# Score matmuls of a decode attention step as four 32-column tiles of the PE array instead of zero-padded 128-column weights

## The chip, the cores and the metric

One core of one Trainium2 chip. The metric is the device time of one execution in microseconds; the kernel before takes 766.4 us (median of 3 runs, 766.21 to 766.55). PE is the matmul engine (TensorE), PEld its weight loads, DVE is VectorE, ACT ScalarE, POOL GpSimd, SP SyncE. The profile counts DMA shares over the core's 16 DMA engines.

## The reference, cut to what matters

Two tokens go through layer norm, a gated attention over the last 4096 positions of a cache of 32768, and a small MLP gate; then come all gradients. Eight key/value heads serve 32 query heads, four each.

```python
W = 4096                                        # of Sk = 32768
k = k_cache[:, :, Sk - W:, :]; v = v_cache[:, :, Sk - W:, :]
scores = einsum("bhqd,bhkd->bhqk", q, k) * Dh**-0.5
p = softmax(scores); o = einsum("bhqk,bhkd->bhqd", p, v)
out = x + (o @ wo) * silu(mlp(xn))              # and the gradients of x, k_cache, v_cache, wq, wo, w1, b1, w2, b2
```

The gradients of the two caches have the caches' full size (2 x 8 x 32768 x 128, bf16). Seven eighths of each are zeros, since only the last 4096 positions are used. These zeros have to be written: they are the bulk of the kernel's traffic.

## The kernel before

The zeros leave as large DMAs from a zeroed tile. POOL issues all regions but one on the software queue, and none of these waits for compute; the last region goes out on SP's queue, after the last result.

```python
sw_fill.append(nc.gpsimd.dma_start(out=v, in_=zs))               # L101, in zf()
...
for qi in range(ZQ - 1):                                         # 31 of 32 regions of 7.34 MB
    ...
        r = zf(*zparts[qi], r, n, rows, rep)
...
last = nc.sync.dma_start(out=out_6..., in_=dw1_st)               # the last result of the compute chain
with tc.issue_after(last.ins):
    fin = nc.sync.dma_start(out=v, in_=zs)                       # the 32nd region
tc.add_manual_dep(fin.ins, sw_fill[-2].ins.name, ...)            # and not before the last fill but one has landed
```

Attention runs in four rounds (two batches, two sets of NP = 4 key/value heads). A round loads 4 MB of V and of K, computes `dp` from V and the scores `s` from K (eight *score passes* in all, two per round), then the softmax, and overwrites the loaded tiles with the cache gradients, which are stored. A score pass takes 16 groups: eight 128x128 transposes, one evacuation (the copy from PSUM, where this kernel's matmuls write, to a ring of four buffers in SBUF, from which they read) by DVE or ACT, and four matmuls, one per head. All heads add into one 128-row accumulator: head `pr` and position group `g` own four of its rows. The weights that put them there are a 128-column window on a zero tile with the head's four query columns in it, so every head's matmul writes zeros on the rows of the other three.

```python
ZO = R - REP                                    # R = 128, REP = 4
ZW = NP * (ZO + R)
zz = const.tile([P, 2 * ZW], BF16, name="zz")   # zeros, with the query (zq) or output-gradient (zdo) columns
nc.vector.memset(zz[:], 0.0)
...
def scores(out_ps, nat, zbuf):
    n = 0
    for half in range(NH):                      # NH = 2
        for g in range(G):                      # G = 8
            tp = ps_t.tile([P, CH, P], BF16, tag="pt")        # 2 buffers in PSUM
            for j in range(CH):                 # CH = 8
                nc.tensor.transpose(tp[:, j, :], nat[:, g * CC + half * CH + j, :], pperm...)      # L384
            tF = tring[:, n % 4 * CH * R:(n % 4 + 1) * CH * R]
            tT = tF.rearrange("p (c b k) -> p c b k", c=CH, b=NP)
            evac(tF, tp..., eng=("act" if n % 4 == 3 else "dve"))
            n += 1
            for pr in range(NP):
                o = ZO - (pr * RB + REP * g)
                nc.tensor.matmul(out_ps[:, half * 256:(half + 1) * 256], lhsT=zbuf[:, pr, o:o + R],
                                 rhs=tT[:, :, pr, :], start=(g == 0 and pr == 0), stop=(g == G - 1 and pr == NP - 1))  # L391
```

## Time and profile before

| | before |
|---|---|
| time | 766.4 us |
| profiled span | 764.5 us |
| bytes moved by DMA | 326.73 MB, of them 227.55 MB on the software queue (nearly all zeros) |
| mean DMA rate | 427 GB/s |
| PE / DVE / ACT busy | 52% / 36% / 28% |
| last compute | 711 us |

First the page of the kernel before: engine totals; the DMA row, which gives the busy share of each fortieth of the span in tenths; the rate in each; and one queue with packets, MB and share of the 16 engines' time.

```profile
span 764.5 us, 9399 instructions
PE 399.7 (52%) x4118; PEld 261.8 (34%) x4118; DVE 275.8 (36%) x483; ACT 214.5 (28%) x313; POOL 35.1 (5%) x67
DMA  9999999999999999999999999999999999999998
GB/s 360 433 425 427 442 422 430 438 426 425 429 428 438 427 446 430 413 427 435 435 427 440 427 433 438 420 433 429 437 430 436 430 440 430 418 438 425 436 417 379
DMA packets 12473, 326.73 MB, mean 427 GB/s; under 512 B 2898, under 2 KB 2906, under 8 KB 2934
q0 software_dynamic: 8000, 227.55, 70.4%
```

The DMA row is the reading that decides this case. It shows 9 tenths in 39 of 40 slices, and the rate stays between 413 and 446 GB/s in all but the first (360) and the last (379), while no compute engine is busy much over half the time (PE 52%). The fills take up what the other queues leave: their queue has 65% of the 16 engines' time from 106 to 134 us, where K is loaded (35%), and 103% from 134 to 157 us, where nothing but small instruction traffic runs beside it; the total is 424 and 432 GB/s.

The score matmuls on the same page (busy us, mean ns of one; then the idle time before them):

```profile
L391 PEld LDWEIGHTS <-zz 128*128 128x128 bf16 x512 | 49.6, 100 | 37.3 <-issue 31.3
L391 PE MATMUL dp_ps<-tring,zz 128*128 128x256 bf16 x256 | 39.2, 284 | 12.1 <-DVE tring L159 6.9
L391 PE MATMUL s_ps<-tring,zz 128*128 128x256 bf16 x256 | 39.0, 275 | 10.9 <-DVE tring L159 9.9
```

Some 275 ns is the recorded length of one matmul, whose end is modelled. What four of them cost is read from the starts. From the timeline of the kernel before, PE alone, inside the first pass over K (start us, busy us):

```profile
139.30 0.60 PE L391 MATMUL s_ps<-tring,zz 128*128 128x256 bf16 x4 [0.34 <-DVE tring L159]
139.73 0.44 PE L384 MATMUL tp<-pperm,nat 128*128 128x128 bf16 x5
140.12 0.60 PE L391 MATMUL s_ps<-tring,zz 128*128 128x256 bf16 x4
140.55 0.78 PE L384 MATMUL tp<-pperm,nat 128*128 128x128 bf16 x11
141.66 0.60 PE L391 MATMUL s_ps<-tring,zz 128*128 128x256 bf16 x4 [0.34 <-DVE tring L159]
```

The transposes start 0.43 us after the first of four score matmuls (139.30 to 139.73). Two groups take 2.36 us (139.30 to 141.66).

Windows of the kernel before: from and to, length, busy us of each engine, granted clock, DMA share, GB/s. (The DMA share adds up the times of packets, so it can pass 1, as it does here with 1.04 and 1.05.)

```profile
134.10:155.70 21.60, 18.09 (x196) 15.21 (x196) 8.29 (x13) 4.05 (x4) 1.72 (x3) 0.93 1.04 435
662.00:711.00 49.00, 37.10 (x112) 14.70 (x111) 32.52 (x45) 18.93 (x33) 0.00 (x0) 0.50 1.05 430
711.00:742.00 31.00, 0.00 (x0) 0.00 (x0) 0.00 (x0) 0.00 (x0) 0.00 (x0) 0.50 1.00 427
```

The first is one whole score pass, 21.6 us. The third has no compute at all and full DMA: compute is finished 53 us before the end of the span.

### The profile page before, as it was taken

The page shows a single profiled execution, that of the slowest core. Times are in us where ns is not written, and L with a number is a line of the kernel's source. Part 1 is how long each engine was busy: PE and PEld are TensorE (multiplying, and loading weights), DVE is VectorE, ACT ScalarE, POOL GpSimd, SP SyncE. Part 2 cuts the span into 40 slices and gives each one's busy share as a digit, 9 for nine tenths or more (in the row PEclk, how much of TensorE's full clock was granted, in tenths as well). Part 3 has the DMA queues.
Part 4 walks back from the last instruction along what each step waited for, and adds up shares of the span by engine and source line. Part 5 has one row for each costly group of instructions (what it writes and reads, how often), then busy time and mean ns, then how long its engine had stood idle before and what let it go on. Part 6 is the DMA issues. An engine that isn't in the chain of part 4 may idle for free.

```text
span 764.5 us, 9399 instructions
## 1 busy us (share of the span) xinstructions
PE 399.7 (52%) x4118; PEld 261.8 (34%) x4118; DVE 275.8 (36%) x483; ACT 214.5 (28%) x313; POOL 35.1 (5%) x67
## 2 busy tenths in 40 slices
PE   0166774848503766870486683017645938759100
PEld 0153363734102654430275430016543424232000
DVE  3034252355501346450254653003343515567100
ACT  0034441145500124560122553002142307316100
POOL 3000010010000000000000000000000000000000
PEclk9998898968755995785599577559876957555555
DMA  9999999999999999999999999999999999999998
GB/s 360 433 425 427 442 422 430 438 426 425 429 428 438 427 446 430 413 427 435 435 427 440 427 433 438 420 433 429 437 430 436 430 440 430 418 438 425 436 417 379
DMA packets 12473, 326.73 MB, mean 427 GB/s; under 512 B 2898, under 2 KB 2906, under 8 KB 2934
## 3 DMA queue, kind: packets, MB, share of 16 engines
q0 software_dynamic: 8000, 227.55, 70.4%
q1 hardware_dynamic: 2696, 56.63, 19.3%
q10 hardware_dynamic: 1736, 41.95, 13.5%
q8 instruction: 32, 0.52, 0.3%
q14 instruction: 9, 0.07, 0.0%
HBM read 45.62 MB, written 280.50 MB: 427 GB/s over the span
## 4 chain that ended last, share of the span: by engine, by line
PE 33%; DMA 32%; DVE 14%; ACT 7%; issue 6%; ACTq 0%; DVEq 0%; SPq 0%
DMA out_dram<-nat 13%; DMA nat<-in_A_v_cache_dram 8%; DMA nat<-in_A_k_cache_dram 8%; PE ov L418 5%; PE s_ps L391 4%; PE tp L384 4%; DMA b_bf<-in_B_b_dram 4%; DVE tring L159 3%; PE dp_ps L391 2%; ACT p_bf L452 2%; ACT nat L157 2%; DVE ds_bf L465 2%; DVE nat L159 2%; PE wps L585 2%; PE ps L407 1%
## 5 line engine op out<-in xcount | busy, mean ns | idle before, releaser
L384 PE MATMUL tp<-pperm,nat 128*128 128x128 bf16 x1024 | 81.9, 228 | 136.4 <-DMA nat<-in_A_v_cache_dram 117.3
L159 DVE COPY tring<-tp 128x1024 bf16<-128x1024 bf16 (+1 forms) x98 | 65.5, 689 | 177.9 <-PE tp L384 168.3
L384 PEld LDWEIGHTS <-nat 128*128 128x128 bf16 x1024 | 70.8, 102 | 142.9 <-DMA nat<-in_A_v_cache_dram 119.3
L157 ACT CAST nat<-ov 128x512 bf16<-128x512 f32 x160 | 87.4, 590 | 61.9 <-PE ov L418 61.2
L157 ACT COPY tring<-tp 128x1024 bf16<-128x1024 bf16 (+1 forms) x34 | 34.4, 1011 | 239.7 <-PE tp L384 223.1
L159 DVE CAST nat<-ov 128x512 bf16<-128x512 f32 x96 | 65.7, 690 | 54.1 <-PE ov L418 51.4
L391 PEld LDWEIGHTS <-zz 128*128 128x128 bf16 x512 | 49.6, 100 | 37.3 <-issue 31.3
L101 POOL DMA_DIRECT2D out_dram<-zt x58 | 33.5, 581 | 529.3 <-DMA out_dram<-zt 526.1
L418 PE MATMUL ov<-bd,ds_bf 128*128 128x512 bf16 x128 | 49.2, 459 | 5.6 <-DVE nat L159 3.7
L418 PE MATMUL ov<-bd,p_bf 128*128 128x512 bf16 x128 | 48.6, 452 | 4.3 <-DVE nat L159 1.4
L391 PE MATMUL dp_ps<-tring,zz 128*128 128x256 bf16 x256 | 39.2, 284 | 12.1 <-DVE tring L159 6.9
L391 PE MATMUL s_ps<-tring,zz 128*128 128x256 bf16 x256 | 39.0, 275 | 10.9 <-DVE tring L159 9.9
L407 PE MATMUL ps<-t,nat 128*128 128x16 bf16 x1024 | 29.0, 174 | 13.7 <-DVE bd L372 6.8
L407 PEld LDWEIGHTS <-nat 128*128 128x128 bf16 x1024 | 28.9, 104 | 16.6 <-issue 11.4
L159 DVE CAST wq<-wps 128x512 bf16<-128x512 f32 x16 | 11.0, 690 | 42.4 <-PE wps L578 42.2
L399 PE MATMUL tp<-ident_bf,p_bf 128*128 128x128 bf16 x64 | 7.5, 312 | 34.9 <-ACT p_bf L452 34.9
L452 ACT ACTIVATE p_bf<-e_sb,rl 32x512 bf16<-32x512 f32 x16 | 22.8, 1424 | 3.4 <-DVE rl L449 3.3
L157 ACT CAST wq<-wps 128x512 bf16<-128x512 f32 x16 | 9.3, 586 | 50.6 <-PE wps L578 50.6
L465 DVE SCALAR_TENSOR_TENSOR ds_bf<-dp_ps,delta,p_bf 32x512 bf16<-32x512 f32 x16 | 21.8, 1360 | 0.2
L418 PEld LDWEIGHTS <-ds_bf 128*128 128x128 bf16 x128 | 12.9, 107 | 20.5 <-issue 18.2
L418 PEld LDWEIGHTS <-p_bf 128*128 128x128 bf16 x128 | 12.7, 108 | 19.5 <-issue 16.4
L399 PEld LDWEIGHTS <-p_bf 128*128 128x128 bf16 x64 | 6.5, 145 | 36.0 <-ACT p_bf L452 36.0
(195 smaller groups left out, 437.6 us busy)
## 6 DMA issues: line engine op xcount, KB each, us to landing
out_dram<-zt POOLq DMA_DIRECT2D x23, 7168.0 KB, 101.3
out_dram<-nat ACTq DMA_DIRECT2D x8, 4096.0 KB, 41.4
out_dram<-zt POOLq DMA_DIRECT2D x7, 3584.0 KB, 63.4
nat<-in_A_v_cache_dram SPq DMA_DIRECT2D x4, 4096.0 KB, 32.6
nat<-in_A_k_cache_dram SPq DMA_DIRECT2D x4, 4096.0 KB, 27.3
out_dram<-zt SPq DMA_DIRECT2D x1, 7168.0 KB, 52.2
out_dram<-zt POOLq DMA_DIRECT2D x2, 3488.0 KB, 64.6
out_dram<-zt POOLq DMA_DIRECT2D x1, 6120.0 KB, 85.8
```

What stands on the lines that cost most here:

```text
L101: sw_fill.append(nc.gpsimd.dma_start(out=v, in_=zs))
L157: nc.scalar.copy(out=out_ap, in_=in_ap)
L159: nc.vector.tensor_copy(out=out_ap, in_=in_ap)
L384: nc.tensor.transpose(tp[:, j, :], nat[:, g * CC + half * CH + j, :], pperm[:].rearrange("p b k -> p (b k)"))
L391: nc.tensor.matmul(out_ps[:, half * CH * PB:(half + 1) * CH * PB], lhsT=zbuf[:, pr, o:o + R], rhs=tT[:, :, pr, :], start=(g == 0 and pr == ...
L399: nc.tensor.transpose(tp[:, cc, :], src[:, half * CH + cc].rearrange("r k b -> r (k b)"), ident_bf[:, :])
L407: nc.tensor.matmul(ps[:], lhsT=nat[:, g * CC + half * CH + cc, :], rhs=cols[half][:, cc, :, g, :], start=(half == 0 and g == 0 and cc == 0 ...
L418: nc.tensor.matmul(ov[:], lhsT=src[:, cc].rearrange("r k b -> r (k b)"), rhs=bd[:, gh * 4:(gh + 1) * 4, :], start=True, stop=True)
L452: nc.scalar.activation(out=p_bf[rb, :, :, pr], in_=e_sb[rb], func=ACT.Copy, scale=rl[rb, 0:1])
L465: nc.vector.scalar_tensor_tensor(out=ds_bf[rb, :, :, pr], in0=dp_c[rb], scalar=delta[rb, 0:1], in1=p_bf[rb, :, :, pr], op0=ALU.subtract, o ...
L585: nc.tensor.matmul(wps[:], lhsT=o_rows[:, j:N:NJ], rhs=ds_rows[:, :], start=True, stop=True)
```

## The change

Each head's weights become 32 columns wide and its output the 32 PSUM partitions that belong to it. The intent is that the four matmuls of a group then run side by side, each as a tile of its own (a column tile: 32 weight columns and the 32 partitions they write), and that three quarters of the multiplications, all by zero, go. The zero tile shrinks from 2016 to 480 columns; three output rows that had borrowed it get a tile of their own. Since the transposes still use all 128 columns, the work on PE changes between 128 columns and tiles of 32 twice in each group; this is called a change of mode below.

```diff
-    ZO = R - REP
-    ZW = NP * (ZO + R)
+    ZO = RB - REP                      # RB = 32
+    ZW = NP * (ZO + RB)
...
-                    o = ZO - (pr * RB + REP * g)
-                    nc.tensor.matmul(out_ps[:, half * CH * PB:(half + 1) * CH * PB], lhsT=zbuf[:, pr, o:o + R], rhs=tT[:, :, pr, :],
-                                     start=(g == 0 and pr == 0), stop=(g == G - 1 and pr == NP - 1))
+                    o = ZO - REP * g
+                    nc.tensor.matmul(out_ps[pr * RB:(pr + 1) * RB, half * CH * PB:(half + 1) * CH * PB],
+                                     lhsT=zbuf[:, pr, o:o + RB], rhs=tT[:, :, pr, :], start=(g == 0), stop=(g == G - 1))
...
+    rows3 = epi.tile([B, 3 * D], BF16, name="rows3")      # and out_rows, db2r, du_rows are cut from it, not from zz
```

More of the change, by code (lines that the diff above doesn't have):

```diff
@@ L498 @@
             tp = to_rows(outT, F32, ident_f[:, :], ps_s, "sd")
-            out_rows = zz[0:B, 0:D]
+            out_rows = rows3[0:B, 0:D]
             nc.vector.tensor_copy(out=pk_rows(out_rows), in_=tp[:])
@@ L506 @@
             nc.vector.tensor_copy(out=db2[:], in_=db2T[:])
-            db2r = zz[0:1, 2 * D:3 * D]
+            db2r = rows3[0:1, 2 * D:3 * D]
             tp1 = ps_s.tile([1, DK, P], BF16, tag="sd")
@@ L514 @@
             tp = to_rows(duT_bf, BF16, ident_bf[:, :], ps_s, "sd")
-            du_rows = zz[0:B, D:2 * D]
+            du_rows = rows3[0:B, D:2 * D]
             nc.vector.tensor_copy(out=pk_rows(du_rows), in_=tp[:])
```

## The prediction

> **What bounds the kernel now.** The DMA engines, not a compute engine. The page moves 326.73 MB in a span of 764.5 us, a mean of 427 GB/s, and its DMA row shows 9 tenths in 39 of 40 slices (the last shows 8); the rate is 413 to 446 GB/s but in the first slice (360) and the last (379). 227.55 MB of it are zero fills on the software queue, which wait for no compute and take what cache loads and stores leave free. PE is busy 52%, DVE 36%, ACT 28%. In windows, PE, DVE and ACT have no work after 712 us, while DMA runs on at 423 to 432 GB/s up to 758 us. The chain of waits names PE for 33%, but all of it lies under full DMA. [...] The change moves no byte more or less.
>
> **What the change does.** Per score group, four matmuls 128x128 by 256 columns (512 matmuls in all, 270 ns each in the record, 97 ns per weight load) become four with 32 weight columns and the same 256 moving columns, into four partition quarters. In the timeline four of them follow each other at about 108 ns and hold PE about 0.43 us; a group of eight transposes, one evacuation and four matmuls takes 1.18 us in the second score pass (139.30 to 141.66 us for two). [...] Estimate from the timeline: if the four overlap, 0.43 us falls to about 0.15 us[...]: net 0 to 0.3 us per group, 0 to 38 us over 128 groups, about 15 us likely. Evacuation (0.69 us on DVE, 1.01 us on ACT per tile) stays and limits the group to little under 1 us.  The smaller zero memset and the new buffer for output rows are off the path.
>
> **On the critical path: almost nothing.** Cache loads and stores start earlier by what PE saves; the zero fills land correspondingly later; the sum of bytes and the rate stay. Even a slower PE would be hidden: about 22 MB are still to move when compute ends at 711 us, so some 20 us of delay should cost nothing.
>
> **Predicted time:** 766.2 us, range 764.0 to 768.5. Faster by over 2%: 0.01; within 2%: 0.97; slower by over 2%: 0.02.
>
> **What would show it.** The DMA row stays at 9 and 425 to 429 GB/s in the mean. The score matmuls start less than 100 ns apart and their weight loads take under 97 ns. A score pass of 16 groups, now 21.6 us (134.1 to 155.7 us), takes 16 to 22 us. The last PE work moves from 711 us to between 690 and 712 us (about 697), and the stretch of DMA without compute grows by as much.
>
> **What would make it wrong.** [...]compute ends more than 20 to 30 us later and the fills run out; a DMA rate that depends on which queues are active together, so that fills alone at the end move slower (or faster) than the mix; an uneven finish of the 16 engines.

The forecast's sum per group was 0.43 us less about 0.15 us (estimate if the four overlap), so 0.28 us saved, less a cost of the changes of mode for which no number stood: net 0 to 0.3 us, or 0 to 38 us over 128 groups, with about 15 us likely. What would have made the forecast wrong: far over 0.5 us of that cost per group, and compute ending more than 20 to 30 us later. The predicted time rests on unchanged bytes at the measured 427 GB/s.

## More of the kernel before

In the timeline, the last store that waits for compute and the last fill follow at once:

```profile
710.84 0.33 SPq L636 DMA_DIRECT2D out_dram<-dw  x1
711.36 0.39 SPq L641 DMA_DIRECT2D out_dram<-zt  x1
```

## The result, and the profile after

| | before | after |
|---|---|---|
| time, median | 766.47 us (4 runs) | 766.44 us (766.23 to 766.53, 4 runs) |
| ratio | | 1.000, 95% interval 0.998 to 1.002 |
| one score pass | 21.6 us | 19.4 us |
| last store that waits for compute is issued at | 710.8 us | 701.0 us |
| last fill is issued at | 711.4 us | 719.1 us |

A ratio is the mean time of one kernel's runs over that of the other's of the same rounds, so not quite the ratio of the medians quoted. Executions over 1.5% slower than the fastest of the same kernel are left out of the means.

The page of the changed kernel:

```profile
span 764.6 us, 9390 instructions
PE 385.0 (50%) x4109; PEld 232.4 (30%) x4118; DVE 275.8 (36%) x483; ACT 214.6 (28%) x313; POOL 35.0 (5%) x67
DMA  9999999999999999999999999999999999999998
GB/s 362 426 428 428 436 419 440 435 429 427 426 428 432 430 448 430 413 428 430 438 426 440 430 427 438 425 426 434 437 433 433 433 418 440 431 425 440 430 416 377
L392 PEld LDWEIGHTS <-zz 128*32 128x32 bf16 x512 | 17.7, 96 | 36.9 <-issue 27.1
L392 PE MATMUL s_ps<-tring,zz 128*32 128x256 bf16 x256 | 19.7, 294 | 14.3 <-ACT tring L157 6.8
L392 PE MATMUL dp_ps<-tring,zz 128*32 128x256 bf16 x256 | 20.2, 322 | 7.7 <-ACT tring L157 4.9
```

Bytes and DMA row are the same. The score matmuls' busy time halves (78.2 to 39.9 us) though one of them is not shorter (294 and 322 ns against 275 and 284): the saving is overlap. The same holds for weight loads, 49.6 to 17.7 us busy at about the same mean length (96 ns against 100). In the timeline of the changed kernel, PE alone:

```profile
139.57 0.29 PE L392 MATMUL s_ps<-tring,zz 128*32 128x256 bf16 x4 [0.38 <-ACT tring L157]
139.79 0.45 PE L385 MATMUL tp<-pperm,nat 128*128 128x128 bf16 x5
140.18 0.29 PE L392 MATMUL s_ps<-tring,zz 128*32 128x256 bf16 x4
140.40 0.79 PE L385 MATMUL tp<-pperm,nat 128*128 128x128 bf16 x11
141.53 0.29 PE L392 MATMUL s_ps<-tring,zz 128*32 128x256 bf16 x4 [0.34 <-DVE tring L159]
```

Four score matmuls now hold PE 0.22 us (139.57 to 139.79) in place of 0.43, and two groups take 1.96 us in place of 2.36. Windows of the changed kernel (the granted clock of the score pass is 0.85, against 0.93 before, so a better clock is not what shortens it):

```profile
133.90:153.30 19.40, 15.08 (x196) 10.46 (x196) 8.14 (x14) 4.05 (x4) 1.71 (x3) 0.85 1.05 438
652.00:702.00 50.00, 37.23 (x113) 14.71 (x111) 32.53 (x45) 19.06 (x33) 0.00 (x0) 0.50 1.07 433
702.00:742.00 40.00, 0.00 (x0) 0.00 (x0) 0.00 (x0) 0.00 (x0) 0.00 (x0) 0.50 1.03 435
```

Compute is done 10 us sooner, and the DMA engines go on as before (435 GB/s from 702 to 742 us). The last fill even goes out later than before, at 719.05 us: it waits for the last software fill but one, which landed at 711.35 us before and lands at 719.04 us now. That the earlier stores have pushed this fill back is the likely reason; it was not tested.

```profile
700.97 0.33 SPq L637 DMA_DIRECT2D out_dram<-dw  x1
719.05 0.39 SPq L642 DMA_DIRECT2D out_dram<-zt  x1
```

**What single starts show.** The instruction starts in the packed trace, taken one by one (the timeline view merges them), give the price of the overlap. Before, the four matmuls of a group start 109 ns apart, 325 ns from first to last. After, they start 3 ns apart, 10 ns in all. But from the last transpose to the first score matmul, where neither had to wait, it is 56 ns before and 149 ns after, and from the last score matmul to the next transpose 109 ns before and 216 ns after (the commonest values). So a group saves 315 ns and pays back 93 + 107 = 200 ns at the two changes of mode: 115 ns net where PE is the limit, or 15 us over 128 groups, an estimate worked out from these starts. Where the first score matmul had to wait for an evacuation anyway, the way into the tiles costs less or nothing: in the two excerpts above the step from the fifth transpose to the next score matmul is 163 ns before and 149 ns after, and there a group gains the whole 0.2 us.

### The profile page after: what moved, and what is told of

The parts are those of the page before. It is cut to its first block, busy times and chain, and to the rows that moved or that the text cites. A ratio compares the mean times of both kernels' runs of the same rounds, so it can differ in the third digit from the quotient of the medians.

```text
span 764.6 us, 9390 instructions
## 1 busy us (share of the span) xinstructions
PE 385.0 (50%) x4109; PEld 232.4 (30%) x4118; DVE 275.8 (36%) x483; ACT 214.6 (28%) x313; POOL 35.0 (5%) x67
## 4 chain that ended last, share of the span: by engine, by line
DMA 33%; PE 32%; DVE 11%; ACT 9%; issue 6%; ACTq 0%; DVEq 0%; SPq 0%
DMA out_dram<-nat 14%; DMA nat<-in_A_k_cache_dram 11%; PE ov L419 7%; PE tp L385 5%; DMA b_bf<-in_B_b_dram 4%; DMA nat<-in_A_v_cache_dram 4%; ACT p_bf L453 2%; PE ps L408 2%; ACT nat L157 2%; ACT tring L157 2%; PE s_ps L392 2%; DVE nat L159 2%; PE wps L586 2%; DVE tring L159 2%; PE dops L312 1%
## 5 line engine op out<-in xcount | busy, mean ns | idle before, releaser
L385 PE MATMUL tp<-pperm,nat 128*128 128x128 bf16 x1024 | 91.2, 241 | 142.5 <-DMA nat<-in_A_v_cache_dram 119.3
L385 PEld LDWEIGHTS <-nat 128*128 128x128 bf16 x1024 | 67.7, 108 | 162.1 <-DMA nat<-in_A_v_cache_dram 121.2
L408 PEld LDWEIGHTS <-nat 128*128 128x128 bf16 x1024 | 28.7, 103 | 16.9 <-issue 11.7
L392 PEld LDWEIGHTS <-zz 128*32 128x32 bf16 x512 | 17.7, 96 | 36.9 <-issue 27.1
L392 PE MATMUL s_ps<-tring,zz 128*32 128x256 bf16 x256 | 19.7, 294 | 14.3 <-ACT tring L157 6.8
L392 PE MATMUL dp_ps<-tring,zz 128*32 128x256 bf16 x256 | 20.2, 322 | 7.7 <-ACT tring L157 4.9
L453 ACT ACTIVATE p_bf<-e_sb,rl 32x512 bf16<-32x512 f32 x16 | 22.8, 1424 | 3.4 <-DVE rl L450 3.2
```

Source lines behind the costliest of these rows:

```text
L392: nc.tensor.matmul(out_ps[pr * RB:(pr + 1) * RB, half * CH * PB:(half + 1) * CH * PB], lhsT=zbuf[:, pr, o:o + RB], rhs=tT[:, :, pr, :], st ...
L408: nc.tensor.matmul(ps[:], lhsT=nat[:, g * CC + half * CH + cc, :], rhs=cols[half][:, cc, :, g, :], start=(half == 0 and g == 0 and cc == 0 ...
L453: nc.scalar.activation(out=p_bf[rb, :, :, pr], in_=e_sb[rb], func=ACT.Copy, scale=rl[rb, 0:1])
```

## The experiments

My theory: the DMA engines bound the whole kernel; the change does shorten the compute chain, and the zero fills hide what it saves. The rivals: the change saves nothing on the chain because the mode changes eat it; or the saving is real but comes from narrower weights and not from tiles side by side; or the chain was critical after all.

### No zero fills: what the change is worth on the compute chain

Both kernels without any fill. Wrong: most of two outputs stays unwritten.

```diff
-    for qi in range(ZQ - 1):
+    for qi in range(0):
...
-    (the last fill on SP's queue and its dependency)
```

> Kernel before without any zero fill (wrong on purpose: most of the two cache gradients is not written). It moves about 92 MB instead of 327. Theory (the DMA engines bound the whole kernel, the compute chain runs hidden under them): the time falls far, and then the chain of loads, compute and stores bounds it, somewhere between 480 and 580 us; the DMA row falls below 9 tenths in most slices. Rival (the compute chain through PE bounds the kernel even now): the time stays above 700 us.

> The changed kernel without zero fills, compared with nf_before. Theory: the change does shorten the score passes (19.4 us against 21.6 us in the traces), and only the zero fills hide it; without them it is 8 to 18 us faster than nf_before, a ratio of 0.965 to 0.985. Rival A (mode changes eat what the tiles save): ratio 0.99 to 1.01. Rival B (both kernels were bound by the compute chain): the ratio is 1.00 as it was with the fills.

Measured: nf_before 582.04 us (580.42 to 583.76, 4 runs), nf_after 563.72 us (561.01 to 564.94, 4 runs). Against the full kernel before, in the same rounds, the ratios are 0.760 (0.758 to 0.762) and 0.735 (0.733 to 0.737); one over the other gives 0.967. The change is worth 18 us, 3.3%, where nothing hides it, at the upper edge of the 8 to 18 us I had expected. From the first transpose to the last score matmul, the eight score passes of the profiled runs take 162.5 us in nf_before and 143.6 us in nf_after (summed from the starts): the gain lies where the change is. Rivals A and B fall. My guess of the time of nf_before (480 to 580) was a little low.

The DMA rows, of nf_before and then of nf_after:

```profile
DMA  8970003300067850005787000479700002466048
```

```profile
DMA  9980001500067770006787000579700003366048
```

Most slices are now well below 9, many at 0: here the chain decides, and here the saving shows. The 184 us between 766 and 582 are what the fills add to the time. They lengthen the chain too: without them the last compute of the kernel before ends at 571.9 us, with them at 710.8. So the slack under the fills is not 184 us; the experiment after the next measures it.

### Three fills fewer: where the hiding ends

```diff
-    for qi in range(ZQ - 1):
+    for qi in range(ZQ - 1 - 3):
```

> Kernel before without the last three of the large software fills (3 times 7.34 MB less; wrong on purpose). If bytes alone bind: 22 MB at 427 GB/s are 51.5 us, so 715 us. My theory: compute ends at 711 us whatever the last fills do, and 11 to 13 MB of stores and the last fill can only follow it (26 to 30 us), so the chain now ends last: 736 to 744 us. If the fills do not matter: 766 us.

> The changed kernel without the same three fills. My theory: its compute ends about 10 us earlier (702 us), so 727 to 735 us, 8 to 12 us below drop3_before: with less filler than the chain needs to hide under, the saving of the change shows. If bytes alone bind: 715 us, equal to drop3_before.

Measured: drop3_before 736.87 us (733.59 to 738.28, 4 runs); drop3_after 729.75 us (725.42 to 736.46, 4 runs, the slowest of which counts as slow; the three fast ones have a mean of 728.3 us, against 736.4 us of drop3_before). The ratios to the full kernel before are 0.961 (0.958 to 0.963) and 0.950 (0.947 to 0.953). Both in the expected ranges, neither at the 715 us of bytes alone, and 8 us apart. The DMA rows of drop3_before and of drop3_after show the hole near the end, where the fills have run out and the last stores are not there yet:

```profile
DMA  9999999999999999999999999999999999998099
```

```profile
DMA  9999999999999999999999999999999999999299
```

So with 7% fewer bytes the same change is worth 1%. Whether it pays is a matter of how much filler there is for the chain to hide under.

### Compute late on purpose: how much slack there is

The changed kernel, complete and right, with serial memsets ahead of the last two weight gradients.

```diff
+    w2flat = w2T[:].rearrange("p k f -> p (k f)")
+    nc.vector.tensor_copy(out=w2flat[:, 0:512], in_=wq[:, DK - 1, N - 512:N])
+    for _ in range(8):                                   # 23 in late70_after
+        nc.vector.memset(w2flat.bitcast(F32), 0.0)       # 3.04 us each
     dw = kvp.tile([P, NCB * DH], BF16, tag="v")
```

> The changed kernel with eight serial memsets (3.05 us each, 24 us) on VectorE ahead of the last two weight gradients; the result stays right. Theory (about 35 us of slack: after the last compute at 702 us there are 62 us of DMA, of which only about 26 us, the last two stores and the last fill, have to wait for compute): compute ends 20 to 28 us later, near 724 us, and the time stays at 766 us, within 0.5%. Rival (the last part of the chain is critical): 786 to 792 us.

> The changed kernel with 23 serial memsets (70 us) on VectorE ahead of the last two weight gradients; the result stays right. Eight of them moved the last compute from 702 to 725 us at no cost, so 23 should move it to about 770 us. Theory: about 35 us of slack; past it the delay is paid one for one, since 26 us of stores and the last fill must follow compute: 790 to 806 us, and the DMA row shows slices below 9 tenths before the end. Rival, a chain that is hidden whatever it takes: 766 us. Rival, no slack left beyond 25 us: 811 us.

Measured: late25_after 766.5 us (766.21 to 766.58), ratio 0.9997 (0.998 to 1.001). Its store of the last weight gradient (L641) is issued at 723.8 us, 22.8 us later than in the changed kernel, the small one of x's gradient (L639) even at 725.1, and this cost nothing. late70_after 802.5 us (799.77 to 804.23), ratio 1.047. There the store is issued at 777.8 us, 76.8 us later, and 36 us of it are paid: about 41 us of slack, an estimate from these numbers that takes what exceeds the slack as paid in full; I had expected 35. SP's DMA issues at the end, of late25_after and then of late70_after:

```profile
723.79 0.33 SPq L641 DMA_DIRECT2D out_dram<-dw  x1
725.12 0.26 SPq L639 DMA_DIRECT2D out_dram<-dw  x1
725.47 1.35 SPq L646 DMA_DIRECT2D out_dram<-zt  x1
```

```profile
777.77 0.33 SPq L641 DMA_DIRECT2D out_dram<-dw  x1
778.20 0.39 SPq L646 DMA_DIRECT2D out_dram<-zt  x1
```

Windows of late70_after show the hole:

```profile
702.00:742.00 40.00, 4.75 (x20) 4.00 (x21) 32.51 (x19) 0.00 (x0) 0.00 (x0) 0.50 1.08 364
742.00:774.00 32.00, 8.42 (x20) 2.42 (x20) 25.12 (x17) 6.28 (x11) 0.00 (x0) 0.50 0.07 29
774.00:801.60 27.60, 3.09 (x8) 0.80 (x6) 2.26 (x5) 2.42 (x5) 0.00 (x0) 0.50 0.87 366
```

From 742 to 774 us the DMA share is 0.07: the fills are gone, and the last stores wait for DVE. A chain that is hidden is hidden up to a point, and past it pays. Two delays bound that point; that each further microsecond costs a whole one is assumed, not shown.

### Tiles side by side, or only narrow weights?

All of these run without fills, so that the chain shows. Three kernels issue the matmuls of four groups as one batch of sixteen; each batch waits for its fourth evacuation, and the order within it is forced. The first is 128 columns wide; the other two use tiles and differ only in order.

```diff
-                for pr in range(NP):                       # after each group
+            # after four groups; the first of the sixteen waits for the fourth evacuation
+            for g, pr in [(g, pr) for g in range(gb, gb + 4) for pr in range(NP)]:     # rot_nf (and wide_nf, 128 wide)
+            for g, pr in [(g, pr) for pr in range(NP) for g in range(gb, gb + 4)]:     # same_nf
```

> No zero fills; score matmuls 128 columns wide as before, but issued sixteen in a row (four groups) instead of four. Control for the next two. In the timeline sixteen matmuls hold PE for about 16 x 108 ns = 1.7 us (at the full clock).

> No zero fills; 32-column tiles, sixteen in a row, in the order that gives each column tile four matmuls in a row. Theory (tiles of different columns run side by side, one tile's matmuls one after the other): these do not overlap but at the three changes of tile, so sixteen hold PE about 1.4 to 1.7 us, near the 128-column control. Rival (narrow weights alone make the matmuls cheap): about 0.5 us.

> No zero fills; the same sixteen 32-column matmuls, with the same mode changes, in rotating order over the four tiles. Theory: four run side by side, so sixteen hold PE about 0.45 to 0.6 us, 1 us less than same_nf; over 32 batches at most 35 us, of which perhaps half lies on the chain: 8 to 25 us less time than same_nf. Rival (narrow weights): the same as same_nf in time and in the timeline.

Measured: wide_nf 591.34 us (587.28 to 592.75), same_nf 564.77 us (564.46 to 564.93), rot_nf 561.56 us (557.58 to 563.47), 4 runs each. One batch from the timeline of wide_nf, of same_nf, and of rot_nf (start us, busy us):

```profile
119.48 1.92 PE L395 MATMUL s_ps<-tring,zz 128*128 128x256 bf16 x16 [0.56 <-ACT tring L157]
121.24 1.06 PE L386 MATMUL tp<-pperm,nat 128*128 128x128 bf16 x16
```

```profile
118.84 0.66 PE L396 MATMUL s_ps<-tring,zz 128*32 128x256 bf16 x16 [0.37 <-ACT tring L157]
119.43 0.62 PE L387 MATMUL tp<-pperm,nat 128*128 128x128 bf16 x8
```

```profile
116.00 0.62 PE L396 MATMUL s_ps<-tring,zz 128*32 128x256 bf16 x16 [0.56 <-ACT tring L157]
116.55 1.15 PE L387 MATMUL tp<-pperm,nat 128*128 128x128 bf16 x16
```

Sixteen wide ones hold PE 1.76 us (119.48 to 121.24), as expected; sixteen in rotating order 0.55 us, as expected; but the order that puts four matmuls of one tile in a row takes 0.59 us, where I had expected 1.4 to 1.7. So the order hardly matters (3 us between the two kernels, where I had expected 8 to 25), and the pair did not tell the two explanations apart. (Tiles against full width does matter: at equal batches rot_nf takes 30 us less than wide_nf. The sixteen weight loads fit into the same stretches: they are busy 1.64 us in wide_nf, 0.37 us in same_nf and 0.34 us in rot_nf.) Either narrow matmuls of one tile overlap too, or PE starts those of another tile past the waiting ones. The single starts speak for the second: in rot_nf fours start together (3 ns apart) every 99 to 109 ns, and in same_nf fours start 13 to 18 ns apart, with 65 to 76 ns to the next four. The views do not say which tile a start belongs to, so one more kernel was needed: one in which there is no second tile.

```diff
-   nc.tensor.matmul(out_ps[pr * RB:(pr + 1) * RB, ...], lhsT=zbuf[:, pr, o:o + RB], ..., start=(g == 0), stop=(g == G - 1))
+   wide = g == 0 and pr == 0                              # gives rows 32 to 127 a value, 16 of 512 matmuls
+   nc.tensor.matmul(out_ps[0:P if wide else RB, ...], lhsT=zz[:, 0:P] if wide else zbuf[:, pr, o:o + RB], ...,
+                    start=wide or (g == 0 and pr == 1), stop=wide or (g == G - 1 and pr == NP - 1))
```

> No zero fills; as nf_after, but all four heads' 32-column matmuls go to the first column tile (wrong on purpose; one 128-column matmul per half pass first gives the other rows a value). Same weights' width, same mode changes, four per group, no second tile to run beside. Theory (tiles side by side are the gain, and mode changes cost about 0.2 us per group): four matmuls start about 109 ns apart again, a group holds PE 0.2 us longer than in nf_before, and the kernel takes 590 to 610 us, slower than nf_before (582). Rival (narrow weights alone are the gain): 560 to 567 us, as nf_after.

Measured: 599.44 us median (594.82 to 605.5, 4 runs; the profiled one, 605.5, counts as slow; the fast ones have a ratio of 0.780, 0.777 to 0.783, to the full kernel before, where nf_before has 0.760 and nf_after 0.735). From its timeline, PE alone:

```profile
121.30 0.60 PE L393 MATMUL s_ps<-tring,zz 128*32 128x256 bf16 x4 [0.34 <-DVE tring L159]
121.83 0.45 PE L385 MATMUL tp<-pperm,nat 128*128 128x128 bf16 x5
```

A group holds PE 0.53 us (121.30 to 121.83), more than the 0.43 us before; with the 93 ns more on the way in, 0.19 us more in all, as expected. The starts are 109 to 119 ns apart again, at the same widths as in nf_after, and the mode changes cost about the same (149 ns into a group, 205 ns out of it). So the gain comes from using several tiles, not from narrow weights. (The four matmuls of one tile also share their PSUM rows; whether the shared columns or the shared rows keep them 109 ns apart, no run separates.) Without a second tile the change would be a loss of about 2.6% on the chain (0.780 over 0.760). And since the matmuls of one tile start 109 to 119 ns apart in onetile_nf, same_nf's sixteen in the program's order would need at least four times three such steps, 1.3 us (an estimate). They hold PE 0.59 us, so PE started other tiles' matmuls past those of the first. One mark in the packed trace shows it directly. In 26 of the 32 batches of same_nf, the program (built again from the run's kernel) has a semaphore update, which tells that a ring buffer is read, on the thirteenth of the sixteen matmuls, the first of the fourth tile. In the trace, the matmul with that update is the fourth to start in all 26, 40 to 45 ns after the first. (The ends in the trace are modelled, so the order of ends stays open.) In rot_nf the same update sits on the program's fourth matmul, and it starts fourth.

Since rot_nf has a quarter of the mode changes of nf_after and yet takes about as long (561.6 against 563.7 us, from different rounds; ratios 0.732 and 0.735), batching is no way to more: it saves mode changes and waits for the fourth evacuation instead (43.7 us of idle time of PE and its weight loads on ACT's evacuations in rot_nf; 12.6 us on ACT's and 8.2 us on DVE's in nf_after). No experiment pointed to a kernel faster than both, since the full kernel's bound is its bytes.

## Why the prediction was right

**The bound, right.** DMA row and rate did not move (427 GB/s in both), and the time is the predicted 766.2 us within 0.3 us. Taking the fills away moved it by 184 us; holding compute back by 22.8 us did not move it at all.

**What the change saves, right in kind and within its range.** Predicted: 0 to 0.3 us per group, some 15 us in all, with overlap as the gain and the changes of mode as the cost (a cost without a number). Measured: 0.115 us net where PE is the limit, 10 us on the last compute in the full kernel, 18 us with the chain laid bare. The estimate was that four matmuls fall to 0.15 us before that cost. Their starts lie 10 ns apart from first to last; with 109 ns for the last one that is about 0.12 us (an estimate), and with the change of mode after them (216 ns to the next transpose, 109 ns before) the group holds PE 0.22 us. The trace gives the sizes of both effects, 3 ns between starts and 200 ns for both changes; what PE does in these 200 ns it does not show.

**The score pass, right:** 19.4 us, predicted 16 to 22. Two groups take 1.96 us, about 0.98 us each; "little under 1 us" was the limit named. Of the evacuations, the 1.01 us one on ACT now ends more of the score matmuls' waits (11.7 us of idle time) than DVE's (6.7 us); before it was the other way round (5.8 and 16.8 us).

**Weight loads, right only in the letter.** Predicted to take under 97 ns: the median is 93 ns, hardly less. What fell is their busy time, by overlap (49.6 to 17.7 us).

**Last compute, right:** about 697 us predicted (690 to 712), the last store that waits for it issued at 701.0 us. The stretch without compute grew from 53 to 63 us.

**Slack, too cautious.** The prediction allowed some 20 us of delay before; the changed kernel has about 41 us, so the kernel before has about 31 us (an estimate: 10 us less). Not on record was the wait of the last fill for the last software fill but one: with compute done sooner it waits until 719 us. It cost nothing: the DMA engines stay full meanwhile (435 GB/s from 702 to 742 us).

## What to carry to other kernels

Before costing a change to an engine, look whether some other resource is full in every slice; here one row (DMA, 9 tenths in 39 of 40 slices) of the profile decided the case, and a change worth 3.3% on the compute chain was worth nothing. To learn what a hidden change is worth, and when it will count, take the covering work away and run both versions, then hold compute back until the time moves: the first gives the gain, the second the slack. And where small column tiles share PE with full-width work, count the changes of mode: here each group of four gained 315 ns by overlap and paid 200 ns for switching.
